# Strassen's seven products for the expert layers of a routed-attention and mixture-of-experts kernel

## The chip, the cores and the metric

The kernel runs on one core of a Trainium2 chip, in float32 but for the one-hot matrices, which are bfloat16. The metric is the device time of one launch in microseconds (us); the kernel before takes 828.1 us, the median of three runs from 826.96 to 828.63. One execution was also profiled (span 827.1 us), and the parts of that profile are shown below as they are printed.

The engines are named as in the profile. PE is TensorE's matmul side, PEld its weight loads, DVE is VectorE, ACT is ScalarE, POOL is GpSimd, and SP issues the large loads. L303 is line 303 of the kernel before.

## What is computed

First comes an attention whose queries and keys are put into 16 clusters for each head; a query attends only to keys of its own cluster. The heads' outputs, side by side, are 3072 rows of 512. Then each row goes to one of eight experts, the one with the largest gate logit. An expert has two layers.

```python
# x: (3072, 512); w1: (8, 512, 1024); w2: (8, 1024, 512)
logits = x @ w_gate
expert_idx = np.argmax(logits, axis=1)
gate_w = softmax(logits)[row, expert_idx]
for e in range(8):
    rows = (rows of x that went to expert e)
    h = np.maximum(x[rows] @ w1[e], 0.0)     # first layer
    y[rows] = h @ w2[e]                      # second layer
out = gate_w[:, None] * y
```

The experts get unequal numbers of rows. The kernel gives each one room for 3 tiles of 128 rows and a remainder of 32, which is 416 rows; whatever exceeds that goes to tiles of 128 rows at the end, of which two are always run.

## The kernel before

The attention fills the first half of the time. While its last batch is still being attended to, the rows of the first three batches are known, and with them the kernel takes early tiles (`groups1`): one tile of 128 rows from each of experts 0, 1 and 2. They keep TensorE at work while VectorE and GpSimd work out which row goes where.

```python
NP = 3
NJ = N // E // P          # 3 tiles an expert
CAP = NJ * P + RQ         # 416 rows
...
def wide():               # PSUM: three buffers of two banks
    return pools["s"].tile([P, 2, 512], F32, name="sps")
```

The first layer has w1 as the stationary operand and the transposed rows as the moving one: 8 blocks of outputs x 4 blocks of the contraction are 32 matmuls whose width is the number of rows.

```python
def layer1(g, fbs):
    cols = sum(g["n"])                      # 416, 288 or 128 rows
    per = min(512 // cols, (fbs[1] - fbs[0]) // 2)
    for f0 in range(fbs[0], fbs[1], 2 * per):
        hp = wide()
        for fb in range(f0, f0 + 2 * per):
            o = hp[:, (fb - f0) // per, ...]
            for c in range(DB):             # DB = 4
                nc.tensor.matmul(o, lhsT=g["w"][0][:, c, fb * P : (fb + 1) * P],
                                 rhs=g["xT"][:, c, :cols], start=(c == 0), stop=(c == DB - 1))      # L303
        for a in range(2):
            if a == 0 and not g.get("scalar_only"):
                nc.vector.tensor_relu(dst, src)                                                     # L311
            else:
                nc.scalar.activation(dst, src, AF.Relu)                                             # L313
```

The second layer works tile by tile. Each tile of 128 rows takes 8 matmuls of 512 columns (L352). The remainder of 32 rows takes 8 matmuls in four column groups of the array (L335), whose four parts are then added (L342 to L345). `rows_out` scales by the gate (L317) and scatters the rows by an indirect DMA (L318).

```python
def layer2(g):
    last = len(g["n"]) - 1
    if g["n"][last] < P:
        ...                                  # 32 rows: L335, then ACT copies and DVE adds of 32 x 512
        rows_out(g, last, RQ, zc[:, 0, :])
    for j, m in enumerate(g["n"]):
        if m < P: continue
        zp = wide()[:, 0, :]
        for fb in range(FB):                 # FB = 8
            nc.tensor.matmul(zp, lhsT=g["h"][:, fb, j * P : (j + 1) * P], rhs=g["w"][1][:, fb, :],
                             start=(fb == 0), stop=(fb == FB - 1))                                  # L352
        rows_out(g, j, P, zp)
```

Between the attention and the experts stands the routing, with the early tiles put in between as filling.

```python
# during the attention's end: first_half(0), the first layer of early tile 0, in three pieces
choose(sm, back)
layer2(groups1[0])
count(back)                                  # L431, L432
...                                          # slots: a chain of small VectorE operations
one_hots(...)  x4                            # VectorE and GpSimd (L462 to L470)
first_half(1)
layer2(groups1[1])
tokens(tok_ps, oh_r, oh_c, NT)               # L477
indices(sm, tok_ps, NC, g_idx, s_idx)
...
first_half(2)
...
for i in range(2): gather_of(groups[i])      # indirect DMAs of the rows
layer2(groups1[2])
turn_of(groups[0])                           # transposes on TensorE, copies on DVE and ACT (L284 to L292)
for i, g in enumerate(groups):               # eight experts and two extra tiles
    g["w"] = weights.pop(i)
    layer1_of(g)
    if i + 1 < len(groups): turn_of(groups[i + 1])
    layer2(g)
    if i + 2 < len(groups): gather_of(groups[i + 2])
    if i + 3 < len(groups): weights[i + 3] = fetch(groups[i + 3]["e"], i + 3)   # 2 MB for w1, 2 MB for w2
```

All of this stage is in a given order: each engine runs its instructions as they are written.

Of the kernel before, what the change touches and what calls it, by code (L numbers as in the profile page):

```python
# [8 lines left out]
F32 = mybir.dt.float32  # L9
# [13 lines left out]
RQ = 32  # L23
NP = 3

# [158 lines left out]
def kernel(  # L184
# [42 lines left out]

    wpools = [wpool, wpool]

    def fetch(e, i):  # L230
        i %= 3
        w1 = wpools[i].tile([P, DB, F], F32, name=f"w1_{i}")
        w2 = wpools[i].tile([P, FB, Dm], F32, name=f"w2_{i}")
        nc.sync.dma_start(out=w1, in_=moe_w1[bass.ds(e, 1)].rearrange("e (a p) f -> p (e a) f", p=P))
        nc.sync.dma_start(out=w2, in_=moe_w2[bass.ds(e, 1)].rearrange("e (a p) d -> p (e a) d", p=P))
        return w1, w2

# [39 lines left out]
    def turn_rows(g):  # L277

        for j0 in range(0, len(g["n"]), 2):
            ms = g["n"][j0 : j0 + 2]  # L280
            tp = wide().rearrange("p a (c t) -> p a c t", t=P)
            for i, m in enumerate(ms):
                for c in range(DB):
                    nc.tensor.transpose(  # L284
                        tp[:, i, c, 0:m], g["xg"][0:m, j0 + i, c * P : (c + 1) * P], ident[0:m, 0:m]
                    )
            for i, m in enumerate(ms):
                dst = g["xT"][:, :, (j0 + i) * P : (j0 + i) * P + m]
                if i == 0:
                    nc.vector.tensor_copy(dst, tp[:, i, :, 0:m])  # L290
                else:
                    nc.scalar.copy(dst, tp[:, i, :, 0:m])  # L292
# [22 lines left out]
    def rows_out(g, j, m, zp):  # L315
        zo = pools["rows"].tile([P, Dm], F32, name="zo", bufs=3)
        nc.scalar.activation(zo[0:m], zp[0:m], AF.Copy, scale=g["xg"][0:m, j, Dm : Dm + 1])  # L317
        ins = nc.gpsimd.indirect_dma_start(  # L318
# [7 lines left out]

    def layer2(g):
        last = len(g["n"]) - 1
        if g["n"][last] < P:

            zq = wide()[:, 0, :]
            n = FB * RQ // P
            for i in range(n):
                for t in range(P // RQ):
                    nc.tensor.matmul(  # L335
                        zq[t * RQ : (t + 1) * RQ, :], lhsT=g["h"][:, t * n + i, last * P : last * P + RQ],
                        rhs=g["w"][1][:, t * n + i, :], start=(i == 0), stop=(i == n - 1),
                    )

            zc = pools["wk"].tile([RQ, P // RQ, Dm], F32, name="zc", bufs=1)  # L340
            for t in range(1, P // RQ):
                nc.scalar.copy(zc[:, t, :], zq[t * RQ : (t + 1) * RQ, :])  # L342
            nc.vector.tensor_tensor(zc[:, 0, :], zc[:, 1, :], zq[0:RQ, :], op=ALU.add)
            for t in range(2, P // RQ):
                nc.vector.tensor_tensor(zc[:, 0, :], zc[:, 0, :], zc[:, t, :], op=ALU.add)  # L345
            rows_out(g, last, RQ, zc[:, 0, :])
        for j, m in enumerate(g["n"]):
            if m < P:
                continue
            zp = wide()[:, 0, :]  # L350
            for fb in range(FB):
                nc.tensor.matmul(  # L352
                    zp, lhsT=g["h"][:, fb, j * P : (j + 1) * P], rhs=g["w"][1][:, fb, :],
                    start=(fb == 0), stop=(fb == FB - 1),
                )
            rows_out(g, j, P, zp)

    def cols_of(t, c0):
# [10 lines left out]
    def place_consts():  # L369
# [10 lines left out]
        nc.gpsimd.memset(firsts, 0.0)  # L380
        nc.gpsimd.memset(firsts[:, 0:NP], float(P))
        k_["b1off"] = iota("b1off", [P, E], [[(NJ + 1) * P, E]], -1, 0)
# [3 lines left out]
        k_["iota"] = iota("iota_f", [P, P], [[1, P]], 0, 0)  # L386
        k_["tiles"] = iota("tiles1", [P, NP], [[NJ + 1, NP]], 0, 0)

# [92 lines left out]
    def indices(pool, ps, w, gi, si):  # L481
# [13 lines left out]
        dict(  # L495
            n=[P], rows=NF * P, e=e, gi=cols_of(g_idx1, e), si=cols_of(s_idx1, e), apart=True, scalar_only=True
        ) for e in range(NP)
    ]
# [3 lines left out]
    with ExitStack() as actx:  # L502
# [370 lines left out]
        def gather1(i):  # L873
            g = groups1[i]
            g["xg"] = p1.tile([P, 1, XW], F32, name="xg1", bufs=NP)
            gather(g)

        def turn_rows1(i):
            g = groups1[i]
            g["xT"] = p1.tile([P, DB, P], F32, name="xT1", bufs=NP)  # L880
            turn_rows(g)

        def first_half(i, f0=0, f1=FB):
            g = groups1[i]
            if f0 == 0:
                g["w"] = weights[i]
                g["h"] = p1.tile([P, FB, P], F32, name="h1", bufs=1)
            layer1(g, (f0, f1))
# [7 lines left out]
        at(n + 4, 1, tokens1)  # L896
        for i in range(NP):
            at(n + 4, 1, gather1, i)
        at(n + 6, 0, turn_rows1, 0)
        at(n + 6, 1, turn_rows1, 1)  # L900
        at(n + 7, 0, turn_rows1, 2)

# [14 lines left out]
        def early(e):  # L917
            weights[e] = fetch(e, e)

# [16 lines left out]
    mctx = ExitStack()  # L936
    wpools.append(mctx.enter_context(tc.tile_pool(name="weights3", bufs=1)))
    weights[2] = fetch(2, 2)
    with tc.tile_pool(name="sm", bufs=1) as sm:
        front, back = parts  # L940
        choose(sm, back)
        layer2(groups1[0])
        count(back)
# [27 lines left out]
        for t0 in range(0, NT, TQ):  # L971
            one_hots(sm, rc, slice(t0, t0 + TQ), k_["iota"], oh_r, oh_c)
        first_half(1)
        layer2(groups1[1])
        tok_ps = ps_m.tile([P, 512], F32, name="mps")[:, 0 : 2 * NC]
# [14 lines left out]
        nc.vector.tensor_reduce(bad[:, 2:3], fit, axis=AX, op=ALU.min)  # L990
        first_half(2)
        bps = ps_m.tile([P, 512], F32, name="mps")[:, 0:1]
# [17 lines left out]

    pools["xg"] = mctx.enter_context(tc.tile_pool(name="moe_x", bufs=3))
    pools["wk"] = mctx.enter_context(tc.tile_pool(name="moe_wk", bufs=2))

# [4 lines left out]
    def turn_of(g):  # L1018
        g["xT"] = pools["wk"].tile([P, DB, CAP], F32, name="xgT")
        turn_rows(g)  # L1020

    def layer1_of(g):
        g["h"] = pools["wk"].tile([P, FB, CAP], F32, name="h_sb")
        layer1(g, (0, FB))

    groups = []
    for e in range(E):
        j0 = 1 if e < NP else 0
        c0 = e * (NJ + 1) + j0
# [5 lines left out]
    for i in range(2):  # L1035
        gather_of(groups[i])
    layer2(groups1[2])
    turn_of(groups[0])
    for i, g in enumerate(groups):
        g["w"] = weights.pop(i)  # L1040
        layer1_of(g)
        if i + 1 < len(groups):
            turn_of(groups[i + 1])
        layer2(g)
        if i + 2 < len(groups):
            gather_of(groups[i + 2])
        if i + 3 < len(groups):
            weights[i + 3] = fetch(groups[i + 3]["e"], i + 3)
    msched.close()
# [4 lines left out]
    with tc.If(more > 0):  # L1054
        nx = nc.values_load(xe[0:1, NX : NX + 1], min_val=0, max_val=NX)
        general = nc.values_load(xe[0:1, NX + 1 : NX + 2], min_val=0, max_val=1)
        with tc.If(nx > XU):
            with ExitStack() as ectx:
# [3 lines left out]
                with tc.For_i(XU, nx, 1) as i:  # L1062
# [4 lines left out]
                    g = dict(  # L1067
                        n=[P], rows=N, w=fetch(ex, 0), gi=lambda j: gi[:, 0:1], si=lambda j: gi[:, 1:2], apart=False
                    )
# [36 lines left out]
```

## Time and profile before

| part of the span | us | what runs |
|---|---|---|
| 0 to 404 | 404 | attention; TensorE busy 394.0, VectorE 275.9 |
| 404 to 456 | 52 | routing, with early tiles between; TensorE busy 48.9 |
| 456 to 557 | 101 | experts 0 to 2, which have 288 rows left |
| 557 to 790 | 233 | experts 3 to 7, 416 rows each |
| 790 to 827 | 37 | two extra tiles and the end |

The borders in the table are read from the timeline, to some us. In the profile, a row of slices gives the busy share of 40 equal pieces of the span in tenths. A group of instructions has a line, an engine, an operation, its operands, their shape and a count; after the bar stand its busy time, the mean duration of one in ns, and the idle time of the engine ahead of it with what ended that. In a timeline, the columns are start, duration, engine, line, operation, operands, count, and in brackets the idle time ahead and its releaser.

Three groups are of use for the cost of elementwise work on VectorE and ScalarE:

```profile
L704 DVE TENSOR_TENSOR T<-T,A 128x768 f32<-128x768 f32 x128 | 122.7, 958 | 14.3 <-ACT lsT L739 0.5
L697 ACT ACTIVATE A<-sps 128x768 f32<-128x768 f32 x192 | 153.1, 811 | 53.2 <-PE sps L695 50.2
L781 DVE TENSOR_TENSOR x<-sps,rd 128x384 f32<-128x384 f32 x32 | 17.6, 553 | 14.3 <-PE sps L778 14.3
```

### The profile page before, as it was taken

How to read it: one execution, taken by the hardware profiler on the slowest of the kernel's cores; microseconds unless marked ns; L12 is line 12 of the kernel's file. 1: busy time of each engine (PE TensorE's matmuls, PEld its weight loads, DVE VectorE, ACT ScalarE, POOL GpSimd, SP SyncE). 2: the span in 40 equal slices, each digit the busy share in tenths (PEclk: the TensorE clock that was granted, in tenths of full speed). 3: DMA queues.
4: the chain of work that ended last, by engine and by line, in shares of the span. 5: the costliest groups of instructions: out<-in, count | busy, mean ns of one | idle time of the engine just before them, and what ended most of it. 6: DMA issues, size and time to landing. Idle time of an engine off the chain costs nothing.

```text
span 827.1 us, 10778 instructions
## 1 busy us (share of the span) xinstructions
PE 802.3 (97%) x4373; PEld 431.8 (52%) x4373; DVE 340.0 (41%) x607; ACT 277.4 (34%) x431; POOL 106.2 (13%) x162
## 2 busy tenths in 40 slices
PE   7999999999999999999999999999999999999994
PEld 4454455555445555444666655745454544545472
DVE  3666776776676677786542112011001020201000
ACT  4564565456546545545311112121112020111100
POOL 2200000000000000021034020221120202020110
PEclk8999999999999999999999999999999999999998
DMA  9027223272242201201432153443243424312010
GB/s 212 0 59 252 67 58 100 59 240 58 58 135 59 57 25 35 97 1 40 153 141 67 58 172 150 163 153 136 112 143 118 168 105 145 137 59 86 27 38 6
DMA packets 76185, 81.67 MB, mean 99 GB/s; under 512 B 52831, under 2 KB 56927, under 8 KB 75616
## 3 DMA queue, kind: packets, MB, share of 16 engines
q1 hardware_dynamic: 70208, 60.82, 24.5%
q0 software_dynamic: 5248, 20.04, 6.6%
q8 instruction: 36, 0.59, 0.3%
q14 instruction: 21, 0.17, 0.1%
q10 hardware_dynamic: 672, 0.05, 0.1%
HBM read 68.26 MB, written 13.68 MB: 99 GB/s over the span
## 4 chain that ended last, share of the span: by engine, by line
PE 45%; issue 39%; POOL 8%; DVE 5%; ACT 1%; POOLq 0%; ACTq 0%; DVEq 0%
PE sps L692 15%; PE O L712 14%; POOL out_dram L318 4%; PE sps L695 4%; POOL xg L272 3%; PE mps L733 3%; PE sps L624 2%; DVE T L704 2%; PE sps L303 2%; PE sps L607 2%; PE sps L778 1%; POOL oh_c L467 1%; PE sps L635 1%; PE mps L746 1%; PE sps L352 1%
## 5 line engine op out<-in xcount | busy, mean ns | idle before, releaser
L303 PE MATMUL sps<-xgT,w 128*128 128x416 f32 (+2 forms) x640 | 174.3, 433 | 1.5 <-issue 1.5
L697 ACT ACTIVATE A<-sps 128x768 f32<-128x768 f32 x192 | 153.1, 811 | 53.2 <-PE sps L695 50.2
L352 PE MATMUL sps<-w,h_sb 128*128 128x512 f32 x368 | 160.6, 595 | 1.2 <-DVE h_sb L311 0.8
L692 PE MATMUL sps<-qk 64*128 64x384 f32 x768 | 160.4, 496 | 0.1
L303 PEld LDWEIGHTS sps<-xgT,w 128*128 128x128 f32 x640 | 111.8, 190 | 65.0 <-issue 55.3
L311 DVE TENSOR_SCALAR h_sb<-sps 128x416 f32<-128x416 f32 (+2 forms) x34 | 18.7, 550 | 280.7 <-PE sps L303 280.7
L712 PE MATMUL O<-A,v_in 128*64 128x384 f32 x768 | 130.9, 490 | 0.0
L704 DVE TENSOR_TENSOR T<-T,A 128x768 f32<-128x768 f32 x128 | 122.7, 958 | 14.3 <-ACT lsT L739 0.5
L352 PEld LDWEIGHTS sps<-w,h_sb 128*128 128x128 f32 x368 | 69.1, 190 | 91.5 <-issue 85.5
L692 PEld LDWEIGHTS sps<-qk 64*128 64x128 f32 x768 | 66.9, 189 | 50.1 <-issue 42.3
L712 PEld LDWEIGHTS O<-A,v_in 128*64 128x64 f32 x768 | 52.3, 137 | 62.4 <-issue 62.3
L318 POOL DMA_INDIRECT out_dram<-zo,s_idx x34 | 33.0, 970 | 309.7 <-ACT zo L317 309.3
L313 ACT ACTIVATE h_sb<-sps 128x416 f32<-128x416 f32 (+2 forms) x34 | 16.5, 484 | 161.3 <-DVE h_sb L311 161.3
L695 PE MATMUL sps<-ohT 64*128 64x384 bf16 x384 | 63.6, 325 | 0.0
L317 ACT ACTIVATE zo<-sps,xg 128x512 f32<-128x512 f32 x26 | 17.9, 687 | 132.3 <-PE sps L352 123.3
L700 DVE SCALAR_TENSOR_TENSOR T<-A 128x768 f32<-128x768 f32 x32 | 30.6, 958 | 49.2 <-ACT A L697 49.2
L645 POOL TENSOR_TENSOR sim<-sim,first_c 128x384 f32<-128x384 f32 x16 | 16.0, 998 | 263.8 <-DVE sim L644 263.8
L720 ACT COPY xT<-O 128x384 f32<-128x384 f32 x32 | 15.4, 483 | 63.9 <-PE O L712 63.9
L272 POOL DMA_INDIRECT xg<-x_rows,g_idx x34 | 32.7, 962 | 20.3 <-issue 9.8
L695 PEld LDWEIGHTS <-ohT 64*128 64x128 bf16 x384 | 19.5, 95 | 25.3 <-issue 0.6
L781 DVE TENSOR_TENSOR x<-sps,rd 128x384 f32<-128x384 f32 x32 | 17.6, 553 | 14.3 <-PE sps L778 14.3
L615 ACT COPY qk<-sps 128x256 f32<-128x256 f32 x16 | 5.9, 372 | 50.6 <-DVE qk L614 50.6
(196 smaller groups left out, 568.4 us busy)
## 6 DMA issues: line engine op xcount, KB each, us to landing
w<-in_moe_w_dram SPq DMA_DIRECT2D x20, 2048.0 KB, 9.4
x_rows<-x POOLq DMA_DIRECT2D x4, 1548.0 KB, 7.8
q_in<-in_q_dram SPq DMA_DIRECT2D x32, 192.0 KB, 4.5
k_in<-in_k_dram SPq DMA_DIRECT2D x32, 192.0 KB, 5.0
v_in<-in_v_dram SPq DMA_DIRECT2D x16, 384.0 KB, 3.4
xg<-x_rows,g_idx POOLq DMA_INDIRECT x34, 7.0
out_dram<-zo,s_idx POOLq DMA_INDIRECT x34, 2.5
csb<-in_centroids_dram ACTq DMA_DIRECT2D x1, 32.0 KB, 1.9
```

Source lines behind the costliest of these rows:

```text
L272: nc.gpsimd.indirect_dma_start(out=g["xg"][0:m, j, :], out_offset=None, in_=x_d[0 : g["rows"], :], in_offset=bass.IndirectOffsetOnAxis(ap= ...
L303: nc.tensor.matmul(o, lhsT=g["w"][0][:, c, fb * P : (fb + 1) * P], rhs=g["xT"][:, c, :cols], start=(c == 0), stop=(c == DB - 1),)
L311: nc.vector.tensor_relu(dst, src)
L318: ins = nc.gpsimd.indirect_dma_start(out=out[:, :], out_offset=bass.IndirectOffsetOnAxis(ap=g["si"](j)[0:m], axis=0), in_=zo[0:m], in_offs ...
L352: nc.tensor.matmul(zp, lhsT=g["h"][:, fb, j * P : (j + 1) * P], rhs=g["w"][1][:, fb, :], start=(fb == 0), stop=(fb == FB - 1),)
L692: nc.tensor.matmul(ps[:, a, 0:HS], lhsT=qk[g][r, 1, ks], rhs=qk[g][r, 0, qs], start=True, stop=False)
L695: nc.tensor.matmul(ps[:, a, 0:HS], lhsT=ohT[g][r, 1, ks], rhs=ohT[g][r, 0, qs], start=False, stop=True)
L697: nc.scalar.activation(A[u], ps[:, :, 0:HS], AF.Exp)
L700: nc.vector.scalar_tensor_tensor(T[g, half], in0=A[u - 1], scalar=1e-9 / P, in1=A[u], op0=ALU.add, op1=ALU.add)
L704: nc.vector.tensor_tensor(T[g, half], T[g, half], A[u], op=ALU.add)
L712: nc.tensor.matmul(O[g, half][a * D : (a + 1) * D, 0:HS], lhsT=rows[g, "v"][:, a, j, :], rhs=a_[:, a, :], start=(j == 0), stop=(j == NQ - 1),)
L733: nc.tensor.matmul(ps[r : r + 32, 0:HS], lhsT=wg[:, g % HP, a, :] if i else one_row, rhs=XT[g][:, half * HS : (half + 1) * HS] if i else t ...
```

## The change

The product of two matrices cut into two by two blocks takes eight block products, or seven in Strassen's form, for which sums of blocks are made before and after. The change uses that form (Winograd's variant, with four sums of each operand's blocks and seven additions of products) for the first layers of experts 1 to 7, and for the first two tiles of their second layers. The aim is to have TensorE stream an eighth fewer columns there, with the sums put on VectorE. The block products have half the rows as their width in the first layer (208 or 144 columns) and half the outputs in the second (256 columns).

```diff
+    def sums_a(s, a11, a12, a21, a22):          # four sums of w1's or h's blocks, all on VectorE
+        tt = nc.vector.tensor_tensor
+        return [ tt(s[0], a21, a22, add), tt(s[1], s[0], a11, subtract),
+                 tt(s[2], a11, a21, subtract), tt(s[3], a12, s[1], subtract) ]      # each as a lambda
+    def sums_b(t, b11, b12, b21, b22): ...      # four sums of x's or w2's blocks, likewise
+
+    def seven(mul, a, s, b, t, u, u3, view, c, ready, steps):
+        def product(x, y):
+            ps = wide()
+            mul(ps, x, y)
+            return view(ps)
+        def more():                             # one sum of the next operands, put in between
+            if steps: steps.pop(0)()
+        c11, c12, c21, c22 = c
+        nc.scalar.copy(u, product(s[1], t[1]))
+        more()
+        p = product(a[0], b[0])
+        add(u, u, p)
+        nc.scalar.copy(c11, p)
+        more()
+        add(u3, u, product(s[2], t[2]))
+        more()
+        p = product(s[0], t[0])
+        add(c12, u, p)
+        add(c22, u3, p)
+        ready(3)
+        more()
+        add(c11, c11, product(a[1], b[2]))
+        ready(0)
+        more()
+        add(c21, u3, product(a[3], t[3]), ALU.subtract)
+        ready(2)
+        more()
+        add(c12, c12, product(s[3], b[3]))
+        ready(1)
+        while steps: more()
...
+    # layer1_s: a product is 4 x 2 matmuls of half the rows; ready(i) is ScalarE's ReLU of block i
+    # pair_s:   a product is 4 matmuls of 256 columns; ready(i) scales a finished tile and scatters it
```

Nothing but the order of the program lets the sums run ahead, so the first layers are moved one expert ahead of the second layers. In each turn of the loop, the first layer of expert i + 1 is run with the sums of expert i's h and w2 in between, then the tile pair of expert i with the sums of expert i + 2's w1 in between, then the transposes and x sums of expert i + 2, and the rest of expert i's second layer.

```diff
     for i, g in enumerate(groups):
-        g["w"] = weights.pop(i)
-        layer1_of(g)
-        if i + 1 < len(groups):
-            turn_of(groups[i + 1])
-        layer2(g)
-        if i + 2 < len(groups):
-            gather_of(groups[i + 2])
-        if i + 3 < len(groups):
-            weights[i + 3] = fetch(groups[i + 3]["e"], i + 3)
+        if i + 1 < ng:
+            n = groups[i + 1]
+            steps = sums_h(g) + sums_w2(g) if by_s(i) else []       # by_s(i): 0 < i < E
+            if by_s(i + 1):
+                layer1_s(n, steps)
+            else:
+                n["scalar_only"] = True
+                for f in steps: f()
+                layer1_of(n)
+        if i + 3 < ng:
+            groups[i + 3]["w"] = [fetch1(groups[i + 3]["e"], i + 3)]
+        n = groups[i + 2] if i + 2 < ng else None
+        steps = sums_w1(n) if by_s(i + 2) else []
+        if by_s(i):
+            pair_s(g, steps)
+            rest = range(2, len(g["n"]))
+        else:
+            rest = range(len(g["n"]))
+        if n is not None:
+            turn_of(n)
+            if i + 4 < ng: gather_of(groups[i + 4])
+            if by_s(i + 2): steps += sums_x(n)
+        for f in steps: f()
+        layer2(g, rest)
+        if n is not None:
+            n["w"].append(fetch2(n["e"], i + 2))
```

The sums take room in SBUF. For it the weights go from three pairs of buffers to two, w1 and w2 being fetched at separate times; the gathered rows go from three buffers to two, with the gate copied out by ScalarE; and other tiles get one buffer in place of two. There are four buffers of output rows in place of three.

The early tiles are two of expert 0 and one of expert 1, in place of one each of experts 0, 1 and 2. So expert 0 has 160 rows left, expert 1 has 288, and all others have 416. The routing part changes with them.

```diff
-NP = 3
+FT = (2, 1)
+NP = sum(FT)
...
         choose(sm, back)
-        layer2(groups1[0])
         count(back)
...
-        first_half(1)
-        layer2(groups1[1])
+        layer2(groups1[0])
         tokens(tok_ps, oh_r, oh_c, NT)
...
-        first_half(2)
+        first_half(1)
...
-    layer2(groups1[2])
-    turn_of(groups[0])
+    (w1 sums of expert 1)
+    layer2(groups1[1])
+    turn_of(groups[0])
+    (first layer of expert 0, in the plain form, with the transposes and x sums of expert 1 at its half)
```

The attention itself, the routing's arithmetic and the two extra tiles' matmuls stay as they are.

## The prediction

> **What bounds the kernel now.** I read the page's forty slices first, then the windows of the expert stage, then the matmul groups by shape, and last the timeline of the routing gap and of the end. The slices:
>
> ```profile
> PE   7999999999999999999999999999999999999994
> DVE  3666776776676677786542112011001020201000
> ACT  4564565456546545545311112121112020111100
> PEclk8999999999999999999999999999999999999998
> ```
>
> TensorE's row is at 9 from the second slice to the last but one. VectorE and ScalarE carry 6 and 5 tenths in the attention half, and 1 or 2 after slice 22 (some 455 us), where the experts run. The windows of four experts of 416 rows say it in numbers (columns: stretch, its length, then busy us and count for PE, weight loads, DVE, ACT, POOL, then clock, DMA share, GB/s):
>
> ```profile
> 557.00:604.00 47.00, 47.00 (x146) 23.50 (x145) 5.78 (x9) 7.43 (x13) 7.99 (x9) 1.00 0.36 128
> 604.00:650.00 46.00, 46.00 (x143) 22.93 (x142) 5.78 (x9) 7.43 (x13) 6.97 (x9) 1.00 0.34 118
> ```
>
> No idle time on PE, full clock, 5.8 us of VectorE in 47. From one expert's first gather to the next (604.33 to 650.99 us in the chain of waits) is 46.66 us. So this stage is a stream of matmuls, and it gets shorter only by fewer streamed columns. But a busy row does not prove that columns are the cost; it could be a fixed cost per instruction or the weight loads. The groups by shape settle that:
>
> ```profile
> L352 PE MATMUL sps<-w,h_sb 128*128 128x512 f32 x368 | 160.6, 595 | 1.2 <-DVE h_sb L311 0.8 <-issue 0.4
> L303 PE MATMUL sps<-xgT,w 128*128 128x416 f32 x320 | 112.5, 512 | 0.0
> L303 PE MATMUL sps<-xgT,w 128*128 128x288 f32 x192 | 47.1, 406 | 1.5 <-issue 1.5
> L303 PEld LDWEIGHTS sps<-xgT,w 128*128 128x128 f32 x640 | 111.8, 190 | 65.0 <-issue 55.3
> ```
>
> Each float32 matmul of the code is two instructions (a first layer of 32 matmuls is x64 in the timeline). What one costs in a stream is the distance of two starts, not the mean of one (512 ns), since they overlap. In the timeline, weight loads at 416 columns start every 0.3495 us and at 512 every 0.430; 64 instructions of 288 take 15.76 us less a tail of 0.16, 0.2437 each; thirty of 128 columns take 3.43 us less the last load's 0.19, over 29 gaps, 0.1117. The line through the ends is 5.6 ns + 0.829 ns per column, and it hits 416 and 288 within 1.5 ns. So columns are the cost, and a load of 190 ns hides even under an instruction that lasts 112 ns. I take from the line: 144 columns 0.125, 160 columns 0.138, 208 columns 0.178, 256 columns 0.218 us.
>
> **What the Trainium skill says.** "TensorE: Matmul & The Clock Gate", section "Back-to-back issue gap", gives N/2.4 + 2.5 ns for an isolated warm matmul: linear with a small floor. The trace agrees in form; a float32 instruction here costs 0.829 ns a column, about twice that slope, and the trace decides. The same page's "LDWEIGHTS (loading the stationary operand)" has P/1.2, 107 ns for 128 columns; here it is 190, and still hidden. "VectorE: DVE Perf Modes", "Mode 2×_2P", says that tensor_tensor cannot use the double-rate mode. The trace agrees: 958 ns for 768 columns in the attention half, 553 for 384, 676 for 512 here, so about 155 ns + 1.04 ns a column. "SBUF — State Buffer", "Who interferes with whom", says that a DVE instruction with two SBUF inputs contends with a GpSimd instruction that reads SBUF. VectorE is nearly idle beside the indirect DMAs of this stage now, so no row shows whether that matters.
>
> **The change, part by part.**
>
> First layers of the six experts with 416 rows: before 64 instructions x 0.3495 = 22.37 us; after 7 products of 16 instructions of 208 columns, 112 x 0.178 = 19.94. Saved 2.43 each, 14.6 together. Columns fall by an eighth (2.80); the 48 further instructions give 0.3 back.
>
> First layer of expert 1 (288 rows): 64 x 0.2437 = 15.60 against 112 x 0.125 = 14.0. Saved 1.6.
>
> Tile pairs of the second layer, experts 1 to 7: 32 x 0.430 = 13.76 against 7 x 8 = 56 of 256 columns, 12.2. Saved 1.57 each, 11.0 together.
>
> Early tiles: two of expert 0 and one of expert 1 in place of one each of experts 0 to 2. First layers of experts 0 to 2, early parts included: before 3 x 7.15 + 3 x 15.60 = 68.25; after 13.93 (256) + 7.15 (128) + 8.84 (160) + 15.60 (288) + 22.37 (416) = 67.9, before Strassen is applied. Saved 0.35. Tiles and 32-row remainders in the second layers stay as many.
>
> PE saved: 14.6 + 1.6 + 11.0 + 0.35 = 27.6 us, 3.3% of 828.1.
>
> What it adds lies on VectorE and ScalarE. Per full expert: w1 and w2 sums 8 x 1024 columns, 1.22 each, 9.8 us; sums of h 4 x 0.69 = 2.8; of x 4 x 0.59 = 2.4; seven adds of 832 columns at 1.02 = 7.2; seven of 256 at 0.42 = 3.0; and the old copies and remainder adds, about 3.5. That is 28.6 us in a period of 46.66 - 2.43 - 1.57 = 42.7, so 67% busy against 12% before, and ScalarE about 12 us (six operations of 832 columns at about 0.87, the rest as now). VectorE does not become the bound on the mean. Its order could still hold PE up, so I laid one period out:
>
> PE has products P1 to P7 of the next first layer every 2.85 us, to 19.9. VectorE first finishes the previous expert's remainder adds (4.1 us into the period, as now: last matmul to last add is about 673.2 to 677.2), then takes one sum and one or two adds per product, is done with P7's add at 21 and with the eighth sum at 23.4. The pair's first product needs the second h sum and the second w2 sum, done at 19.4: 0.5 us to spare. Its third needs the third w2 sum at 22.2, wanted at 23.5. There are three PSUM buffers of two banks; none is wanted before its reader is done (P4 at 8.5 wants P1's, free at 5.7). DVE and ACT writes to h come one after the other already (line 313 of ScalarE is released by line 311 of VectorE 34 times); chained like that, ScalarE's ReLU and the next add still fit in 2.85 us. So I expect no wait in experts 2 to 6.
>
> Where PE should wait:
> - Expert 1's turn (after its pair comes only the 1.85 us remainder): next x sums done about 4.7 after the pair, remainder done at 3.7. About 1 us.
> - Expert 7: eight sums stand before the short first layer of extra 8 (7.2 us), but VectorE reaches the second w2 sum at 4.1 + 2.8 + 2.4 = 9.3. About 2 us.
> - Routing gap. The lines now:
>
> ```profile
> 413.87 7.03 PE L352 MATMUL sps<-w,h 128*128 128x512 f32 x16
> 420.74 0.28 PE L431 MATMUL mps<-pr_b,lt_strict 128*128 128x8 f32 x2
> 421.10 7.39 PE L303 MATMUL sps<-xT,w 128*128 128x128 f32 x64
> 429.24 7.13 PE L352 MATMUL sps<-w,h 128*128 128x512 f32 x16 [0.75 <-ACT h L313]
> 436.21 1.04 PE L477 MATMUL mps<-oh_c,oh_r 128*128 128x108 bf16 x18
> 437.43 0.45 PE L477 MATMUL mps<-oh_c,oh_r 128*128 128x108 bf16 x6 [0.19 <-POOL oh_c L467]
> ```
>
> Between the count (420.7) and the last tokens (437.4) stands a chain on VectorE and GpSimd, and PE fills it with one early first layer and one early second layer, 15 us. After, the early expert's 256-column first layer is about 6.8 us longer ahead of the count, but the 7 us second layer ahead of it is gone; the count stays near 421. The fill is then two second-layer tiles, 13.8 us. About 1.3 us of new wait, less the 0.75 in the lines.
>
> Given back: 1 + 2 + 0.6, about 3.6. At the end a second layer no longer follows its own first layer at once, so the waits of 0.39 and 0.78 us ahead of lines 352 at 794 and 809 us go: 1.2 regained. I add 1.5 for what I did not see. 828.1 - 27.6 + 3.6 - 1.2 + 1.5 = 804.4; I say **804 us**.
>
> **The rivals.** (a) VectorE's order holds PE up in each period. For it: the 0.5 us to spare at the pair's start, and rows already chained DVE to ACT; VectorE at 67%. Against: 14 us of slack in a period. Two us in each of seven periods would make 818. (b) Small instructions do not follow at the line's rate, because the loads (190 ns) now exceed the matmul (178). For it: the load row is 24 of 47 us now and would be 168 x 0.19 = 32 us for the Strassen parts alone in 42.7. Against: the 128-column stream at 0.1117. If it held, each of the 6 x 112 = 672 instructions of 208 columns would cost 0.19: 672 x 0.012 = 8 us back, 812. (c) Transfers: w1 buffers go from three to two. Each 2 MB takes 9.4 us to land and has over 20 us; hidden. The tightest is expert 2's w1, fetched as expert 1's 14 us first layer starts. If it were late, some 3 us once. (d) Contention of VectorE's sums with GpSimd would lengthen sums or gathers; both have slack, so 1 to 2 us.
>
> **Range and chances.** Rivals (a) and (b) in part, and several small waits, are likelier than a further gain; below 797 there is nothing in the sum, since 800.5 is PE with no new wait and the tail's 1.2 brings 799.3. I take 797 to 816. The 2% line is at 811.5; (a) at about 1 us a period stays under it. Chances: faster 0.82, same 0.15, slower 0.03.
>
> **What would show it.** Right: groups of 208 and 256 columns with starts 0.178 and 0.218 us apart, periods of 42.7 us with PE full, VectorE near 29 us in each, count near 421 us. Wrong: repeated waits of PE on w2s, xs or u rows of VectorE in each period (a), load starts 0.19 apart (b), or a wait on a weight DMA (c).

## The result and the profile after

| | median us | lowest to highest | ratio to before, 95% interval |
|---|---|---|---|
| before | 828.02 | 826.96 to 828.63 | |
| changed, first measurement | 802.47 | 800.37 to 804.30 | 0.969 (0.966 to 0.972) |
| changed, second measurement | 801.66 | 800.53 to 803.37 | 0.967 (0.966 to 0.968) |

The changed kernel is 3.1% faster, 1.5 us under the predicted 804. The profile below is of an execution that took 804.3 us, the longest of its four. Its forty slices:

```profile
PE   6999999999999999999999899999999999999994
DVE  3667667767667767787536336867484847471610
ACT  4554654554655554645510123232323232232120
PEclk8999999999999999999999999999999999999998
```

TensorE's row looks as before, full from the second slice to the last but one, but for an 8 in slice 23. What is new is VectorE's row in slices 25 to 36: 4 to 8 tenths where it was 0 to 2. The sums have gone into a place that was empty. Two whole turns of the loop in windows (stretch, its length, then busy us and count for PE, weight loads, DVE, ACT, POOL, then clock, DMA share, GB/s):

```profile
613.99:656.55 42.56, 42.56 (x220) 35.31 (x216) 26.71 (x35) 11.54 (x19) 4.85 (x6) 1.00 0.33 118
656.55:699.12 42.57, 42.57 (x220) 35.32 (x217) 26.71 (x35) 11.54 (x19) 4.83 (x6) 1.00 0.35 125
```

A turn takes 42.57 us in place of 46.66, PE has no idle time in it and the clock is full. VectorE carries 26.7 us of work (63%) where it carried 5.8 in 47. Since PE is still never idle, the whole 4.09 us of a turn are matmul time that is gone. The matmul groups by shape, and the costliest of the new adds:

```profile
L363 PE MATMUL sps<-w,h_sb 128*128 128x512 f32 x144 | 63.6, 596 | 0.0
L475 PEld LDWEIGHTS sps<-xs,w1s 128*128 128x128 f32 x336 | 56.4, 190 | 5.7 <-issue 5.7
L475 PE MATMUL sps<-xs,w1s 128*128 128x208 f32 x288 | 53.2, 341 | 0.6 <-DVE xs L385 0.6
L497 PE MATMUL sps<-w2s,hs 128*128 128x256 f32 x168 | 38.6, 379 | 1.8 <-DVE w2s L385 1.8
...
L431 DVE TENSOR_TENSOR h_sb<-h_sb,sps 128x832 f32<-128x832 f32 x12 | 12.3, 1021 | 5.9 <-PE sps L475 3.9 <-ACT h_sb L490 2.0
```

Line 475 is the first layers' seven products, 497 the tile pairs', 363 the plain second layer, 309 the plain first layer, 431 the adds of products, and 377, 378, 385 and 386 the sums. Further on, 290 is the transposes, 296 and 298 their copies on VectorE and ScalarE, 317 and 319 the plain ReLUs on VectorE and ScalarE, and 642 the token matmuls. An add of 832 columns takes 1.02 us, as estimated. The mean of one matmul (341 ns) is again not its cost. The timeline of PE in one turn gives that by the distance of starts (start, us, engine, line, operation, count, and in brackets the idle time ahead of it):

```profile
630.97 2.98 PE L475 MATMUL sps<-xgT,w1s 128*128 128x208 f32 x16
633.78 1.89 PE L497 MATMUL sps<-w2s,hs 128*128 128x256 f32 x8
635.51 1.89 PE L497 MATMUL sps<-w,h_sb 128*128 128x256 f32 x8
637.24 3.62 PE L497 MATMUL sps<-w2s,hs 128*128 128x256 f32 x16
```

Sixteen instructions of 208 columns take 633.78 - 630.97 = 2.81 us, 0.1757 each. Eight of 256 columns take 1.73, 0.216 each. A weight load still lasts 190 ns, longer than the 176 ns that an instruction costs, and it does not slow the stream. The same turn on VectorE:

```profile
632.11 1.22 DVE L385 TENSOR_TENSOR w2s<-w,w2s 128x1024 f32<-128x1024 f32 x1
633.99 1.02 DVE L431 TENSOR_TENSOR h_sb<-h_sb,sps 128x832 f32<-128x832 f32 x1 [0.66 <-PE sps L475]
634.92 1.22 DVE L386 TENSOR_TENSOR w2s<-w 128x1024 f32<-128x1024 f32 x1
```

The first line is the second w2 sum, which the pair's first product reads. A sum takes 1.22 us, as estimated; it ends at 632.11 + 1.22 = 633.33, and the product starts at 633.78: 0.45 us to spare. The last line is the third w2 sum, for the pair's third product: ended at 636.14, wanted at 637.24. What PE did wait for from the routing gap on, in the list of waits (us in total, times, longest):

```profile
PE sps L309 <- ACT h_sb L319: 1.9, 1, 1.9
PE sps L497 <- DVE w2s L385: 1.8, 1, 1.8
PE mps L642 <- POOL oh_c L632: 1.5, 1, 1.5
PE sps L309 <- issue: 1.1, 1, 1.1
...
PE sps L475 <- DVE xs L385: 0.6, 1, 0.6
PE sps L363 <- ACT hs L319: 0.6, 1, 0.6
```

Each stands once, and none comes back every turn. The 1.1 and the last 0.6 have their counterparts in the kernel before (1.5 and 0.6). Of the others, the first is the only one that the prediction did not have. In the timeline of PE it stands in the two halves of expert 0's plain first layer:

```profile
454.45 4.61 PE L309 MATMUL sps<-xu,w 128*128 128x160 f32 x32 [1.08 <-issue]
458.90 1.40 PE L290 MATMUL sps<-ident,xg 128*128 128x128 f32 x12
462.15 6.29 PE L309 MATMUL sps<-xu,w 128*128 128x160 f32 x32 [1.85 <-ACT h_sb L319]
468.27 2.12 PE L475 MATMUL sps<-xs,w1s 128*128 128x144 f32 x16
```

The same 32 instructions take 4.45 us in the first half (start to start) and 6.12 in the second, right after a wait of 1.85. The windows of that stretch say why (columns as above):

```profile
463.50:465.00 1.50, 1.50 (x8) 1.50 (x7) 1.06 (x3) 0.00 (x0) 1.21 (x1) 0.50 0.52 118
465.00:466.50 1.50, 1.50 (x8) 1.50 (x8) 0.00 (x0) 0.00 (x0) 0.97 (x2) 0.62 0.55 151
466.50:468.20 1.70, 1.70 (x15) 1.70 (x14) 0.00 (x0) 0.00 (x0) 0.88 (x1) 1.00 0.54 202
```

PE is busy, but the granted clock falls to 0.50 (called half clock from here on), and fewer instructions go through (8 in 1.5 us against 15 in 1.7). So the wait cost 1.85 us and then 1.7 more.

### The profile page after: what moved, and what is told of

It reads as the page before. It is cut to its first block, busy times and chain, and to the rows that moved or that the text cites. A ratio compares the mean times of both kernels' runs of the same rounds, so it can differ in the third digit from the quotient of the medians.

```text
span 802.5 us, 11975 instructions
## 1 busy us (share of the span) xinstructions
PE 774.7 (97%) x4813; PEld 505.5 (63%) x4813; DVE 484.0 (60%) x783; ACT 307.1 (38%) x479; POOL 110.1 (14%) x164
## 4 chain that ended last, share of the span: by engine, by line
PE 74%; issue 12%; DVE 7%; POOL 3%; ACT 2%; POOLq 0%; ACTq 0%; DVEq 0%
PE sps L858 15%; PE sps L475 14%; PE O L878 13%; PE sps L497 8%; PE sps L363 4%; PE sps L309 4%; PE sps L861 3%; DVE T L870 3%; PE mps L899 3%; PE sps L790 2%; PE sps L290 2%; PE sps L773 2%; POOL out_dram L327 1%; PE sps L944 1%; PE mps L912 1%
## 5 line engine op out<-in xcount | busy, mean ns | idle before, releaser
L363 PE MATMUL sps<-w,h_sb 128*128 128x512 f32 x144 | 63.6, 596 | 0.0
L475 PEld LDWEIGHTS sps<-xs,w1s 128*128 128x128 f32 x336 | 56.4, 190 | 5.7 <-issue 5.7
L475 PE MATMUL sps<-xs,w1s 128*128 128x208 f32 (+1 forms) x336 | 59.4, 333 | 0.6 <-DVE xs L385 0.6
L490 ACT ACTIVATE h_sb<-h_sb 128x832 f32<-128x832 f32 (+1 forms) x28 | 24.3, 867 | 69.8 <-DVE h_sb L431 69.8
L363 PEld LDWEIGHTS sps<-w,h_sb 128*128 128x128 f32 x144 | 26.7, 190 | 30.8 <-issue 30.6
L273 POOL DMA_INDIRECT xg<-x_rows,g_idx x34 | 36.6, 1078 | 38.5 <-ACT xgT L298 17.1
L497 PE MATMUL sps<-w2s,hs 128*128 128x256 f32 x168 | 38.6, 379 | 1.8 <-DVE w2s L385 1.8
L475 PE MATMUL sps<-xgT,w 128*128 128x208 f32 (+1 forms) x224 | 40.0, 331 | 0.0
L475 PEld LDWEIGHTS sps<-xgT,w 128*128 128x128 f32 x224 | 38.0, 190 | 0.0
L351 DVE TENSOR_TENSOR zc<-zc,sps 32x512 f32<-32x512 f32 x8 | 5.4, 675 | 53.6 <-ACT zc L350 53.6
L323 ACT ACTIVATE zo<-sps,gate 128x512 f32<-128x512 f32 x12 | 8.3, 688 | 73.9 <-PE sps L363 49.7
```

What stands on the lines that cost most here:

```text
L273: nc.gpsimd.indirect_dma_start(out=g["xg"][0:m, j, :], out_offset=None, in_=x_d[0 : g["rows"], :], in_offset=bass.IndirectOffsetOnAxis(ap= ...
L475: nc.tensor.matmul(o, lhsT=a[:, c, f * P : (f + 1) * P], rhs=b[:, c, :], start=(c == 0), stop=(c == KH - 1),)
L497: nc.tensor.matmul(ps[:, 0, 0:DH], lhsT=a[:, f, :], rhs=b[:, f, :], start=(f == 0), stop=(f == FH - 1),)
```

## The experiments

The theory: the time falls by the columns that TensorE no longer streams, less a few single waits; VectorE's sums are free as long as each is done before its product. The main rival: VectorE's order sets part of each turn. All edits below are to the changed kernel.

**1 to 3: the three parts apart.** One kernel has the order and the early tiles alone; one has seven products in the first layers alone; one has them in the pairs alone.

```diff
 # order and early tiles only (the w1 and x sums of expert 1 ahead of the loop are cut too)
-    by_s = lambda i: 0 < i < E
+    by_s = lambda i: False
 # first layers only
-            steps = sums_h(g) + sums_w2(g) if by_s(i) else []
+            steps = []
...
-        if by_s(i):                     # pair_s
+        if False:
 # pairs only (all sums of w1 and x cut)
-            if by_s(i + 1):             # layer1_s
+            if False:
```

> The plain forms of both layers in the new order, with the new early tiles and buffers: no Strassen product and no sums. Theory (the gain is streamed columns): by the changed kernel's trace an instruction of 208, 144 and 256 columns takes 0.1757, 0.1225 and 0.2159 us, so Strassen saves 6 x (22.37 - 112 x 0.1757) + (15.60 - 112 x 0.1225) + 7 x (13.76 - 56 x 0.2159) = 16.1 + 1.9 + 11.7 = 29.7 us, less two waits on sums of 0.6 and 1.8; taken out, 802.5 + 27.3 = 830, slightly slower than the kernel before. Rival (the order and the early tiles bring a part of the gain themselves): 815 to 824.

> Strassen in the first layers alone; second layers plain, no sums of h and w2. Theory: the pairs are worth 11.7 us and cost the wait of 1.8 us at expert 7, so 802.5 + 9.9 = 812. Rival (VectorE's order holds TensorE up, so that fewer sums give something back): under 809.

> Strassen in the tile pairs alone; first layers plain with the ReLU on ScalarE, no sums of x and w1. Theory: first layers are worth 18.0 us and cost a wait of 0.6, so 802.5 + 17.4 = 820. Rival (as before): under 816.

| | us | ratio to before |
|---|---|---|
| order and early tiles | 826.52 (825.31 to 828.74) | 0.9985 (0.9977 to 0.9994) |
| and first layers | 808.99 (808.72 to 809.84) | 0.978 (0.976 to 0.980) |
| and pairs | 816.76 (815.79 to 816.95) | 0.987 (0.985 to 0.989) |

Over the order alone, the first layers bring 826.52 - 808.99 = 17.5 us and the pairs 826.52 - 816.76 = 9.8. The products' own terms at the measured distances are 18.0 (six of 2.69 and one of 1.88) and 11.7 (seven of 1.67); of the latter, a wait of 1.8 at expert 7 goes off, which stands in the list of waits of the kernel with pairs alone. So nearly all of what PE no longer streams is gained, and the moved order by itself brings next to nothing. The 808.99 just meets the rival's mark of 809, but that kernel's list has no wait on VectorE from the routing gap on. Both together should bring 27.3, to 799.2. The changed kernel took 802.5. Each kernel came out some 3 us under what I expected of it, since those figures were worked from the changed kernel's time. The missing 3 us are in the changed kernel: none of these three profiles shows the late wait at expert 0. That is the question of experiments 7, 9 and 12.

**4: VectorE's h sums made twice.** This puts 2.8 us more VectorE work into a turn that has 16 us free, ahead of the w2 sums.

```diff
-        return sums_a(g["hs"], *a_of2(g))
+        return [f for f in sums_a(g["hs"], *a_of2(g)) for _ in range(2)]
```

> Each of the four sums of h is made twice: 4 x 0.69 = 2.8 us more of VectorE in each of seven turns, 29.5 of 42.6 us. Theory (the place in VectorE's order decides, not its mean load): the second w2 sum, ready 0.45 us before the pair's first product wants it, comes up to 2.8 us later, so TensorE waits some 2 us in each of the turns of experts 1 to 6 and 2.8 more at expert 7: 802.5 + 12 to 18 = 815 to 820, more if the clock sinks after the waits. Rival (a third of VectorE is idle and takes it up): within 2 us of the changed kernel, except at expert 7.

It took 850.24 us (849.16 to 854.67), ratio 1.029 (1.026 to 1.032): 48 us more than the changed kernel, where I had expected 12 to 18, or more if the clock fell. The timeline of PE in a turn of it:

```profile
598.25 2.98 PE L475 MATMUL sps<-xgT,w1s 128*128 128x208 f32 x16
606.16 3.75 PE L497 MATMUL sps<-w2s,hs 128*128 128x256 f32 x8 [4.93 <-DVE w2s L385]
609.70 3.00 PE L497 MATMUL sps<-w,h_sb 128*128 128x256 f32 x8
612.54 3.62 PE L497 MATMUL sps<-w2s,hs 128*128 128x256 f32 x16
```

And VectorE ahead of that wait:

```profile
601.27 1.02 DVE L431 TENSOR_TENSOR h_sb<-h_sb,sps 128x832 f32<-128x832 f32 x1 [1.19 <-PE sps L475]
602.21 1.41 DVE L378 TENSOR_TENSOR hs<-h_sb,hs 128x512 f32<-128x512 f32 x2
603.53 1.22 DVE L385 TENSOR_TENSOR w2s<-w 128x1024 f32<-128x1024 f32 x1
604.79 1.22 DVE L385 TENSOR_TENSOR w2s<-w,w2s 128x1024 f32<-128x1024 f32 x1
```

VectorE is not short of time: it idles 1.19 us waiting for PE's seventh product. But one sum is taken per product, and there are seven products. Four more h sums push every w2 sum behind the seventh product's add (601.27 us). So the sum that PE needs at 601 is begun at 604.79, and PE stands still for 4.93 us. In the list of waits this row is 34.2 us in 7 times, where it was 1.8 in the changed kernel:

```profile
PE sps L497 <- DVE w2s L385: 34.2, 7, 4.9
```

That is only part of it. The first two products then take 6.38 us from 606.16 to 612.54, in place of 637.24 - 633.78 = 3.46. The windows:

```profile
606.10:609.70 3.60, 3.54 (x8) 2.86 (x9) 3.31 (x3) 0.00 (x0) 0.00 (x0) 0.50 0.00 0
609.70:612.50 2.80, 2.80 (x9) 2.30 (x8) 0.00 (x0) 0.37 (x1) 0.00 (x0) 0.60 0.00 0
```

Half clock again, after each wait. The seven pairs lose 15.6 us to it together, which with the 32.4 us of added waits makes 48.0. The two profiles differ by 847.4 - 802.5 = 44.9; this one reaches the count 2.3 us earlier (418.04 against 420.33) and loses 1.9 us less at expert 0, which leaves 43.8 of the 48.0. My expectation failed on the slots (I had counted VectorE's free time, not the turns in which sums are taken), and it had no figure for the clock.

**5: the w1 sums made twice.** The same doubling for w1's sums, 4.9 us per turn, but behind the point where PE waits for w2.

```diff
-        return sums_a(g["w1s"], *a_of1(g))
+        return [f for f in sums_a(g["w1s"], *a_of1(g)) for _ in range(2)]
```

> Each of the four sums of w1 is made twice: 4 x 1.22 = 4.9 us more of VectorE in each turn, nearly twice what the doubled h sums added, but between the pair's products, where the next thing that waits for VectorE (the first product of the next first layer) comes 9 us after the pair. Theory (place, not load): within 3 us of the changed kernel, with a wait at expert 1's turn alone, where no full tile follows the pair. Rival (VectorE has no more room than the 2.8 us showed): 40 us or more slower.

It took 809.38 us (806.78 to 812.25), 7 us more than the changed kernel, with a ratio to before of 0.978 (0.975 to 0.981). In the turns of experts 2 to 6 it has no wait, as expected, and the rival's 40 us did not come. But it is more than the 3 us that I had allowed. The 7 us come from the edges, of which I had only expert 1's turn. From its list of waits:

```profile
PE sps L475 <- DVE xs L385: 5.0, 2, 2.8
PE sps L309 <- ACT xu L298: 3.2, 1, 3.2
```

At expert 0 the w1 sums of expert 1 stand ahead of copies that PE needs. At the loop's start no pair precedes expert 2's sums, and in expert 1's turn only the remainder follows the pair. There the extra sums reach PE, by 3.2, 2.8 and 2.2 us, and half clock follows: behind the wait of 2.22 us, expert 3's first product took 4.39 us in place of 2.81.

**6: experiment 4's instructions in another order.** The h sums are still made twice, but two w2 sums go ahead of the second half of them.

```diff
-            steps = sums_h(g) + sums_w2(g) if by_s(i) else []
+            sh, sw = sums_h(g), sums_w2(g)
+            steps = sh[:4] + sw[:2] + sh[4:] + sw[2:]
```

> The same doubled h sums, instruction for instruction, but in another order: h0 h0 h1 h1 w0 w1 first, then h2 h2 h3 h3 w2 w3. What the pair's first product wants is then ready after six sums, as in the changed kernel; its third product may wait up to 1 us. Theory (the program puts one sum behind each product, so the number of sums ahead of the wanted one is what counts): 802 to 810. Rival (VectorE's work as such made 850): 840 or more.

It took 811.11 us (811.09 to 811.17), 39 less than experiment 4 with the same instructions. It lies 1 us above the range that I had given. The ratio to before is 0.980 (0.979 to 0.982). From its waits on VectorE in the expert stage:

```profile
PE sps L497 <- DVE w2s L386: 9.3, 6, 1.5
...
PE sps L497 <- DVE w2s L385: 2.0, 1, 2.0
```

The first product no longer waits; the third now does, 1.54 us in each of six turns, for the third w2 sum. A turn takes 44.35 us (569.29 to 613.64), 1.8 more than 42.57: the wait and little else, with no loss of clock behind it. The order of VectorE decides, not its load. Experiment 4 is rival (a) of the prediction made real by 2.8 us of work in the wrong place.

**7, 9 and 12: the wait at expert 0.** The ReLU of the first half is done late there. On VectorE (changed kernel):

```profile
461.14 0.49 DVE L317 TENSOR_SCALAR h_sb<-sps 128x320 f32<-128x320 f32 x1 [7.04 <-PE sps L290]
```

Its matmuls were done at 454.45 + 4.61 = 459.06, and VectorE had been idle for 7 us. ScalarE's ReLU follows it, and PE's second half follows that. At this place the kernel issues the gathers of experts 2 and 3. Experiment 7 issues them after expert 0's first layer; experiment 9 is the changed kernel once more, and 12 is experiment 7 once more.

```diff
     turn_of(g)
-    gather_of(groups[2])
     layer1(g, (0, FB // 2))
     turn_of(groups[1])
-    gather_of(groups[3])
     for f in sums_x(groups[1]): f()
     layer1(g, (FB // 2, FB))
+    gather_of(groups[2])
+    gather_of(groups[3])
```

> The gathers of experts 2 and 3 are issued after expert 0's first layer in place of within it. In the changed kernel's trace VectorE's first ReLU there begins 2.0 us after its matmuls are done, just as the gathered rows of expert 2 have landed; TensorE waits 1.85 us and then runs at half clock for some 3 us. If the gathers hold that ReLU, it begins at once here, and the time is 3 us less: 799. If not: 802 to 803, with the same wait in the trace.

> The changed kernel itself once more. Its four times so far lie at 800.4, 801.4, 803.5 and 804.3, those of the other kernels within 1 to 2 us. Theory (the wait ahead of expert 0's second half comes in some executions and not in others, and costs some 3.5 us with the half clock behind it): single times near 799 to 801 and near 803 to 804; a profile without that wait has a span near 797 to 799. Rival (it comes always, and the gathers make it): all times 802 to 804.

> e7 once more, beside e11 on the same chip. Theory (with those gathers out of expert 0's first layer its ReLU starts in time in every execution): single times within 798.3 to 800, no wait on that ReLU in the profile. Rival (the late ReLU comes now and then whatever the gathers do): one or two times 3 us higher.

| | us | ratio to before |
|---|---|---|
| 7, gathers late | 799.14 (798.51 to 799.71) | 0.966 (0.965 to 0.968) |
| 9, changed again | 801.66 (800.53 to 803.37) | 0.967 (0.966 to 0.968) |
| 12, gathers late again | 798.89 (798.32 to 799.82) | 0.965 (0.964 to 0.967) |

In experiment 7 the ReLU starts as its matmuls end (456.84), and the line on VectorE names them:

```profile
456.88 0.49 DVE L317 TENSOR_SCALAR h_sb<-sps 128x320 f32<-128x320 f32 x1 [5.00 <-PE sps L309]
```

From the first half's start to the first product of expert 1, the changed kernel takes 468.27 - 454.45 = 13.82 us and experiment 7 takes 462.46 - 452.23 = 10.23. The 3.6 us are the wait and the half clock. The medians differ by 3.3 and, in the second pair, 2.8. The other 2.2 us between these two profiles come from ahead of the count (420.33 against 418.11), in the attention half: in the changed kernel's profile the clock is 0.50 from 15.6 to 22.4 us, in experiment 7's it is 1.00 there. The profile of the kernel before has the same fall, so it does not come from the change.

So moving the gathers removes the wait: all nine executions lie between 798.3 and 799.8, and all nine of the changed kernel at 800.37 or above. What holds the ReLU up is not settled. The late ReLU stands in the profiles of the changed kernel, of its repetition (1.81 us) and of experiment 4, but not in those of experiments 1, 2, 3, 5 and 6, which have the gathers in the old place too. So the gathers' place alone is not enough for it. In the three late ones it begins within 0.2 us of the end of the last DMA packet of expert 2's gather (461.14 and 461.09 in the changed kernel); in experiment 6 it begins 2.3 us ahead of that end. A cause is not shown by this.

The times of experiment 9 fit neither of its two pictures: 801.66 and 801.68 lie between the groups. The mean clocks on record say more. The three fastest executions of the changed kernel, 800.37 to 800.60 us, have 0.996 or 0.997. Four executions with the gathers late have 0.996 too, and took 798.32 to 798.89. So the changed kernel takes 1.5 to 2.3 us more at no lower clock, about the wait of 1.85 alone; its slowest three, 803.37 to 804.30, have 0.990 to 0.992. This fits a ReLU that is late in each execution and a clock that falls behind it in some. With two of the nine profiled, it is not shown.

**11: expert 7's sums one turn earlier, with the gathers late.**

```diff
-            steps = sums_h(g) + sums_w2(g) if by_s(i) else []
+            steps = sums_h(g) + sums_w2(g) if by_s(i) and i != E - 1 else []
...
+        if i == E - 2:
+            steps += sums_h(groups[i + 1]) + sums_w2(groups[i + 1])
         for f in steps: f()
         layer2(g, rest)
```

> The gathers of experts 2 and 3 late, as in e7, and the eight sums of expert 7 made one turn earlier, behind expert 6's pair, where no sums of w1 are left to make. The wait of 1.8 us ahead of expert 7's pair goes, and nothing new waits: 1.8 us less than e12 beside it, some 797.3. If VectorE then comes late for expert 6's remainder: no gain.

It took 797.25 us (796.43 to 797.92), ratio 0.963 (0.962 to 0.964). The sums are now made while PE runs the rest of expert 6's second layer, and the wait of 1.77 us at expert 7 is gone from the timeline:

```profile
735.89 7.41 PE L309 MATMUL sps<-xgT,w 128*128 128x128 f32 x64
743.14 1.89 PE L497 MATMUL sps<-w2s,hs 128*128 128x256 f32 x8
```

With 799.14 and 798.89 for the gathers alone, these sums bring 1.6 to 1.9. This version beats the changed kernel by 5.2 us.

**8 and 10: the routing gap filled.** Experiment 8 has the gathers late and expert 7's sums early, makes expert 0's first layer whole, and also fills the gaps around the tokens. Experiment 10 is the same with one result in a PSUM buffer of its own.

```diff
-        layer2(groups1[0])
+        layer2(groups1[0], [0])              # one early tile here, the other after the tokens
+        first_half(1)                        # expert 1's early first layer ahead of the tokens
+        (the test of the denominators, with its matmul, here too)
         tokens(tok_ps, oh_r, oh_c, NT)
...
+        layer2(groups1[0], [1])
...
 # experiment 10, beside this
-        bps = ps_m.tile([P, 512], F32, name="mps")[:, 0:1]
+        bps = ps_o.tile([P, 512], F32, name="O")[:, 0:1]
```

> An attempt at a faster version: the early first layer of expert 1 stands ahead of the last token matmuls, one early second-layer tile after them; the check of the denominators is made earlier, so that the gathers start about 4 us sooner; the transposes of experts 0 and 1 follow each other, and expert 0's first layer is in one piece with its ReLU on ScalarE; expert 7's sums are made one turn earlier. Waits of 1.5, 1.1, 1.9 (with some 1.7 of half clock behind it) and 1.8 us should go and at most 1.5 come new: 802.5 - 8.0 + 1.5 = 796. If the waits only move: 800 to 803.

> The attempt at a faster version again, with the check's one-column result in a PSUM buffer of its own, so that the token matmuls don't wait for VectorE to read it: the wait of 1.4 us ahead of them shrinks to some 0.6. 796.4; same as e8 if the gathers' landing then takes up what is won.

Experiment 8 took 797.22 us (796.3 to 799.84), ratio 0.965 (0.963 to 0.967), as expected, but no better than experiment 11, which does far less. From the count to the first product of expert 1 it takes 463.21 - 419.01 = 44.20 us, and experiment 7, with nothing filled, 462.46 - 418.11 = 44.35. The waits only changed their names: 1.48 for the tokens, 0.63 and 1.08 in experiment 7; in experiment 8 the tokens wait 1.41 for a VectorE operation of that test, and the transposes 1.6 for the gathered rows. What it gains over experiment 7 is about what expert 7's sums, moved in it too, bring alone.

I took the PSUM buffer that the test shares with the tokens for the cause, and gave the test its own. Experiment 10 then took 801.13 us (800.94 to 806.4), ratio 0.969 (0.967 to 0.972): a miss. Its waits from 420 to 480 us:

```profile
PE sps L309 <- issue: 1.9, 5, 0.6
PE mps L642 <- POOL oh_c L632: 1.6, 1, 1.6
PE sps L290 <- DMA xg<-x_rows,g_idx: 1.4, 2, 0.7
```

The tokens wait as long as before, now for the one-hot rows again, so these were due at the same time. And expert 0's first layer has five gaps in which PE waits for nothing visible, at a clock of 1.00; it takes 466.86 - 454.56 = 12.30 us in place of 8.80 in experiment 8. The 3.5 us are most of the 3.9 between the two medians. PE is not alone in it: ScalarE's ReLU of the layer's first half begins at 466.36, in experiment 8 at 459.06, and VectorE's first copy of expert 1's rows at 456.14 against 454.16. The cause is open.

## Why the prediction was right

**Columns are the cost.** This held, and rival (b) with it fell: 208-column instructions follow at 0.1757 us, under the 0.190 of a load, and 256-column ones at 0.216. The line through 128 and 512 columns gave 0.178 and 0.218, some 2 ns too much each. Over 112 and 56 instructions that makes the products' saving 29.7 us (6 x 2.69 + 1.88 + 7 x 1.67) where I had 27.2. This is the larger of two mis-sized terms.

**A turn without a wait.** Predicted 42.7 us, measured 42.57. VectorE carried 26.7 us against my 28.6. The pair's first product had 0.45 us to spare where I had 0.5. The third w2 sum was done 22.15 us into the turn (636.14 - 613.99) and its product began at 23.25, where I had 22.2 and 23.5.

**Rival (a)** did not come about, and experiments 4 and 6 show how near it lay. A slack of 0.45 us was enough, but my argument "14 us of slack in a period" was worth nothing: in experiment 4 VectorE had plenty of slack as well.

**The single waits.** Tokens: 1.48 for 1.3. Expert 1's turn: 0.63 for 1. Expert 7: 1.77 for 2. The count at 420.3 for "near 421". The two waits at the tail are gone.

**Rivals (c) and (d).** No row of waits names a weight transfer. The gathers' issue on GpSimd went from 962 to 1078 ns in the mean. Experiment 1, which has the new order but no sums and no adds of products on VectorE, has 961 (first line: changed kernel):

```profile
L273 POOL DMA_INDIRECT xg<-x_rows,g_idx x34 | 36.6, 1078 | 38.5 <-ACT xgT L298 17.1
...
L273 POOL DMA_INDIRECT xg<-x_rows,g_idx x34 | 32.7, 961 | 131.1 <-ACT xgT L298 112.3
```

Experiment 3, without the sums of x and w1, has 962. So the lengthening comes with VectorE's added work in the first layers; single gathers last up to 1.96 us. This agrees with the Trainium skill, "SBUF — State Buffer", section "Who interferes with whom", as the prediction quotes it. PE never waited for it in the changed kernel.

**What I did not see.** I had 1.5 us for it. The late ReLU at expert 0 cost 1.85 and the half clock behind it 1.7, together some 3.5. Summed with measured terms: 828.1 - 29.7 - 0.35 + 0.7 (tokens, less the 0.75 before) + 0.6 + 1.8 - 1.2 = 799.9, which is experiment 7's 799.1 within a microsecond; with 3.5 it is 803.4, against 802.5. So the mechanism was right, and two terms were off by 2.5 and 2.0 us in opposite directions. That the prediction lay within 1.5 us is partly luck.

## What to carry to other kernels

Whether a helper engine holds up TensorE is read from where the awaited operation stands in the helper's order, not from its busy share: lay out one period and note the slack at each product. Price matmuls by the distance of starts, fitted over shapes that the profile already has. Watch single waits of some 1.8 us or more on TensorE, since the clock may sink behind them and nearly double their cost.

## What the runs showed of the hardware

The granted clock fell to 0.50 behind waits that are short. Here are the waits looked at, with what was lost after each:

| wait of PE, us | kernel | lost in the products or layer half behind it, us |
|---|---|---|
| 1.54, six times | experiment 6, third product | none |
| 1.58 | experiment 4, expert 0 | none |
| 1.77 or 1.78, six profiles | changed, its repetition, experiments 3, 5, 7 and 12, expert 7 | none |
| 1.81 | changed again, expert 0 | 1.6 |
| 1.85 (1.08 eight us earlier) | changed, expert 0 | 1.7 |
| 2.02 | experiment 6, expert 7 | 1.8 |
| 2.22, 2.78, 3.20 | experiment 5, its three | 1.8, 1.6, 1.7 |
| 4.67 to 4.93 | experiment 4, seven pairs | 1.5 to 3.0 |

A fall lasts 3.4 or 6.8 us (462.7 to 466.15 in the changed kernel, 553.9 to 560.7 in experiment 4), and it does not begin with the wait. In experiment 4 the clock falls at 512.95, 553.91, 605.11 and 656.31 us, which are 12, 15 and 15 times 3.413 us apart, while the waits there end at 513.35, 556.17, 606.16 and 656.74.

The Trainium skill, "TensorE: Matmul & The Clock Gate", section "Part 1: The HAM clock gate", has the half clock after an idle window of about 3.4 us, and says that the window runs freely and does not restart with the kernel. The lengths and distances of the falls agree with such a window. But these runs show the half clock behind waits of 1.81 us already. The boundary between 1.78 and 1.81 may be chance: where a wait lies in the window may count beside its length, and no run here varies the place alone.
